# A sparse attention with a gated network behind it: the second chunk's exponentials stay in PSUM, four output buffers, and another order at two places

## The chip, the core and the metric

The kernel runs on one core of one Trainium2 chip. A core has five engines with a queue each: TensorE (PE, whose weight loads are listed as PEld), VectorE (DVE), ScalarE (ACT), GpSimd (POOL) and SyncE (SP). SP issues most of the DMA transfers, POOL some. The metric is the device time of one execution in microseconds (us), as a median over executions. PSUM is the memory that PE writes its results to, in banks of 128 partitions by 512 floats; SBUF is the large memory on the chip.

## The reference, cut to what matters

```python
# q, k, v: 8 batches x 8 heads x 576 positions x 64; 8 global positions
scores = scale * np.matmul(q, k.transpose(0, 1, 3, 2))
mask = np.abs(pos[:, None] - pos[None, :]) <= 32
mask = mask | is_global[:, None] | is_global[None, :]
scores = np.where(mask, scores, -1000000000.0)
attn = softmax(scores)
x = attn @ v                       # regrouped as 4608 tokens x 512
g = x @ w_gate                     # 512 -> 1536
ffn_out = gelu(g) * (x @ w_val) @ w_out
out = x + sigmoid(x @ w_res) * ffn_out
```

Each token attends to its neighbours within 32 positions and to 8 global positions; the global positions attend to all. The result goes through a gated network and is added back under a second gate.

## The kernel before

**Tiles and chunks.** The 4608 tokens are worked through in nine chunks (number c, 0 to 8) of 512, that is, eight windows of 64 query positions. A chunk has four token tiles (t, 0 to 3) of 128. For a chunk, the attention gives `xtok` (tokens by features), which is transposed into `xt` (`turn_x`, L591). The network is then computed from `xt`: for each of twelve blocks j of the hidden width, a gate product and a value product (`ffn_in`, L602; matmuls at L618), a Gelu on ACT (L624) and a product on DVE (L625) that gives `ht`. The output half (`ffn_out`, L629) has for each token tile a residual gate (L636, L639) and three thirds of the last product (L661). After the third one DVE forms `prb` (L665), POOL adds the tokens and gives `ob` (L667), and SP sends `ob` to the output (L669). The attention of chunk c + 1 is placed between the pieces of the output half of chunk c.

**What sets the order.** The order is written out by hand: instructions stand on each engine in the order in which the program names them, and every engine works its own list in order. Between engines there are waits: for an operand, or for a buffer that is still in use. Buffers of one tag take turns: `ob` and `prb` have two each, the PSUM tag "mm" four banks, the tag "sc" two banks, and the pair of banks "nd" exists once.

**The attention of a chunk.** `scores` (L533) computes for half of the windows (a "quad") four banks of scores, two from "sc" and two from "mm". `weigh` (L528) takes the exponential on ACT and writes it to `pt` in SBUF as bf16. `mask` (L543) multiplies `pt` by the window mask on DVE (L545). `local_values` (L551) multiplies `pt` with V into a value sum `nd`, `values` (L567) adds the part of the global positions (L575), which needs `vgs` from `global_rows` (L488, L503), and divides (L581 and L582 for tiles 0 and 2 of chunk 0, L587 and L588 else). In chunk 0 the mask is added by PE ahead of the exponential instead (`first_scores`, L508).

**The start (L732 to L773).** For chunk 0 the value sums of three tiles are begun ahead (`begun_v`), with a copy on ACT (L734) in between. Then values, transposes (`turn_x`) and the first two blocks of gate and value products take turns tile by tile; `begin(t)` is these products for tile t, 16 small matmuls that need the transposed tile t, which ACT copies out of PSUM (L599; DVE for tile 3).

**The end of chunk 0 (L853 to L894).** Here the attention of chunk 1 is placed between the output pieces of chunk 0 by hand. `third(t, n)` is one third of the output product of tile t. In the same place the K and Q of batch 2 are loaded (L199), cast (L205, K on ACT, Q on POOL) and transposed by DMA on SP (`turn_qk`, L461, five transfers for each of K and Q; `qt` and `kt` are their destinations).

**The next chunk.** At the beginning of chunk 1, SP transposes Q of batch 2, and POOL issues the loads of V (L99) and three indirect gathers of global rows of K, Q and V (`gather`, L326, issued at L328) into `kgf`, `qgf`, `vgf`. After block 9 the gathered K and Q are transposed on PE (`turn_globals`, L402, L407), after a cast on DVE (L397). After block 11, `global_scores` (L468) uses `qt` and `kt`. At block 8 POOL's loads of batch 3 into `q_st` and `k_st` are issued (`load_qk`, L87).

The last tile of all is finished by `ending` (L641) in three pieces of 256, 128 and 128 columns, each with its own `prb` (L650), `ob` (L653) and output transfer (L654).

Of the kernel before, what the change touches and what calls it, by code (L numbers as in the profile page):

```python
# [8 lines left out]
F32 = mybir.dt.float32  # L9
# [3 lines left out]
ACTF = mybir.ActivationFunctionType  # L13
ALU = mybir.AluOpType


def view(t, p0, pn, off, dims):

    step = t.ap[0][0]
    return bass.AP(tensor=t.tensor, offset=t.offset + p0 * step + off, ap=[[step, pn]] + dims)  # L20
# [3 lines left out]
def kernel(  # L24
# [12 lines left out]
    nc = tc.nc  # L37
# [4 lines left out]
    SCALE = 1.0 / float(D) ** 0.5  # L42
# [14 lines left out]
    work = ctx.enter_context(tc.tile_pool(name="work", bufs=2))  # L57
# [144 lines left out]
    def cast_second(what, r0, r1, copy):  # L202
        for r in range(r0, r1):
            n = min(128, S - 128 * r)
            copy({"q": q_st, "k": k_st}[what][0:n, r, :], place2[what][r][0:n, :])  # L205
# [255 lines left out]
    def turn_qk(b, parts="qk"):  # L461
        for what in parts:
            src, dst, c0 = (q_st, qt[b % 2], 0) if what == "q" else (k_st, kt[b % 2], 32)
            for r in range(NQT):
                n = min(128, S - 128 * r)
                nc.sync.dma_start(dst[:, :, c0 + 128 * r:c0 + 128 * r + n], src[0:n, r, :], transpose=True)
# [58 lines left out]
                                     qt[b % 2][64 * u:64 * u + 64, 2 * pp + m, 64 * i:64 * i + 64],  # L525
                                     start=first, stop=first or (m == 1 and n == 3))

    def weigh(quad, pp, u, sc):  # L528
        mine = view(pt, 0, 128, ((4 * pp + u) * CH + 4 * quad) * 128, [[2 * CH * 128, 2], [128, 4], [1, 64]])
        nc.scalar.activation(mine, sc, ACTF.Exp, bias=0.0, scale=SCALE)  # L530
        return mine

    def scores(c, quad):  # L533

        i0 = (CH * c + 4 * quad) % NW
        banks = []
        for pp, pool, tag in ((0, pss, "sc"), (1, psm, "mm")):
            sc = [pool.tile([128, 2, 4, 64], F32, name="sc", tag=tag) for _ in range(2)]
            heads(c, quad, pp, sc, True)
            banks += [(pp, u, sc[u]) for u in range(2)]  # L540
        mine = [weigh(quad, *which) for which in banks]

        def mask(n0, n1):  # L543
            for m in mine[n0:n1]:
                nc.vector.tensor_tensor(m, m, view(maskw, 0, 128, 64 * i0, [[0, 2], [64, 4], [1, 64]]), ALU.mult)  # L545
        return mask

    def split(c, t):
# [2 lines left out]
    def local_values(c, t):  # L551
        if split(c, t):
            nds = [psm.tile([128, 512], F32, name=f"nd{hf}", tag="mm") for hf in range(2)]
            nd = None
        else:
            nd = psn.tile([128, 2, 512], F32, name="nd", tag="nd")
            nds = [nd[:, 0, :], nd[:, 1, :]]
        wins = [divmod(CH * c + 2 * t + e, NW) for e in range(2)]
        for h in range(H):
            for e, (b, i) in enumerate(wins):  # L560
                vw = ve[b % 2][:, i // 2, h, :] if i % 2 == 0 else vo[b % 2][:, i // 2, h, :]
                c0 = (h * CH + 2 * t + e) * 128 - 64 * e
                nc.tensor.matmul(nds[h // 4][:, VG * (h % 4):VG * (h % 4) + VG],  # L563
                                 view(pt, 0, 128, c0, [[1, 128]]), vw, start=(h % 4 == 0 and e == 0), stop=False)
        return nd, nds, wins
# [25 lines left out]
    def turn_x(c, t):  # L591
        mine = xt[c % 2][:, :, 128 * t:128 * t + 128]
        if c > 1 and t < 3:
            nc.sync.dma_start(mine, xtok[c % 2][:, t, :], transpose=True)
            return
        tx = pss.tile([128, NKT, 128], BF16, name="tx", tag="sc")
        for kk in range(NKT):
            nc.tensor.transpose(tx[:, kk, :], xtok[c % 2][:, t, 128 * kk:128 * kk + 128], ident)
        (nc.vector.tensor_copy if c or t == 3 else nc.scalar.copy)(mine, tx)  # L599
# [29 lines left out]
    def ffn_out(c, t):  # L629

        held = {}

        def gate():
            r_ps = psm.tile([128, 512], F32, name="r_ps", tag="mm")
            for kk in range(NKT):
                nc.tensor.matmul(r_ps, xt[c % 2][:, kk, 128 * t:128 * t + 128], wr_t[:, kk, :],  # L636
                                 start=(kk == 0), stop=(kk == NKT - 1))
            held["r"] = work.tile([128, 512], BF16, name="rsb", tag="rsb", bufs=4)
            nc.scalar.activation(held["r"], r_ps, ACTF.Tanh, bias=0.0, scale=0.5)  # L639

        def ending():  # L641

            r0 = 512 * c + 128 * t
            for c0, c1 in ((0, 256), (256, 384), (384, 512)):
                f = psm.tile([128, 512], F32, name="f_ps", tag="mm")
                for j in range(NFF):
                    nc.tensor.matmul(f[:, 0:c1 - c0], ht[:, j, 128 * t:128 * t + 128], wo_t[:, j, c0:c1],
                                     start=(j == 0), stop=(j == NFF - 1))
                prb = work.tile([128, 512], F32, name="prb", tag="prb")
                nc.vector.scalar_tensor_tensor(prb[:, c0:c1], held["r"][:, c0:c1], 1.0, f[:, 0:c1 - c0],  # L650
                                               ALU.add, ALU.mult)
                ob = work.tile([128, 512], F32, name="ob", tag="ob")
                nc.vector.tensor_tensor(ob[:, c0:c1], prb[:, c0:c1], xtok[c % 2][:, t, c0:c1], ALU.add)  # L653
                nc.sync.dma_start(out[r0:r0 + 128, c0:c1], ob[:, c0:c1])  # L654

        def third(n):
            def emit():
                if n == 0:
                    held["f"] = psm.tile([128, 512], F32, name="f_ps", tag="mm")
                for j in range(4 * n, 4 * n + 4):  # L660
                    nc.tensor.matmul(held["f"], ht[:, j, 128 * t:128 * t + 128], wo_t[:, j, :],  # L661
                                     start=(j == 0), stop=(j == NFF - 1))
                if n == 2:
                    prb = work.tile([128, 512], F32, name="prb", tag="prb")
                    nc.vector.scalar_tensor_tensor(prb, held["r"], 1.0, held["f"], ALU.add, ALU.mult)  # L665
                    ob = work.tile([128, 512], F32, name="ob", tag="ob")
                    nc.gpsimd.tensor_tensor(ob, prb, xtok[c % 2][:, t, :], ALU.add)  # L667
                    r0 = 512 * c + 128 * t
                    nc.sync.dma_start(out[r0:r0 + 128, :], ob)  # L669
            return emit  # L670

        if c == NCH - 1 and t == 3:
            return [gate, ending, lambda: None, lambda: None]
        return [gate, third(0), third(1), third(2)]
# [57 lines left out]
    begun_v = [local_values(0, t) for t in range(2)]  # L732
    global_rows(0)
    ACT(vo[0][0:64, 2:4, :, :], ve[0][64:128, 2:4, :, :])  # L734
    begun_v.append(local_values(0, 2))

    nc.scalar.activation(none, none, ACTF.Gelu, bias=0.0, scale=1.0)
    for n in range(4):
# [18 lines left out]
    def begin(t):  # L757
        for steps in begun:
            for what in "gv":
                steps[what](128 * t, 128 * t + 128)  # L760

    values(0, 2, begun_v[2])
    turn_x(0, 0)
    values(0, 3)
    turn_x(0, 1)
    begin(0)
    turn_x(0, 2)
    begin(1)
    turn_x(0, 3)
    begin(2)  # L770
    begin(3)
# [8 lines left out]
    for c in range(NCH):  # L780
# [72 lines left out]
        if c == 0:  # L853
            def third(t, n):
                work_f[4 * t + 1 + n]()

            global_exp(1, *global_scores(1))
            work_f[0]()
            scores(1, 0)(0, 4)
            work_f[4]()  # L860
            work_f[8]()
            mask = scores(1, 1)
            work_f[12]()
            global_rows(1)
            for what in "kq":
                load_second(what)
            cast_second("k", 0, NQT, ACT)
            began = local_values(1, 0)
            third(0, 0)
            values(1, 0, began)  # L870
            mask(0, 2)
            third(1, 0)
            values(1, 1)
            mask(2, 4)
            third(2, 0)
            turn_x(1, 0)
            third(3, 0)
            values(1, 2)
            turn_x(1, 1)
            third(0, 1)  # L880
            cast_second("q", 0, 1, POOL)
            values(1, 3)
            third(1, 1)
            cast_second("q", 1, 3, POOL)
            turn_qk(2, "k")
            turn_x(1, 2)
            third(2, 1)
            third(3, 1)
            turn_x(1, 3)
            for t in range(4):  # L890
                third(t, 2)
                if t == 1:
                    cast_second("q", 3, NQT, POOL)
            continue  # L894
        jobs = {n: [] for n in range(16)}
        if c + 1 < NCH:
# [48 lines left out]
```

The softmax here doesn't subtract the row's maximum and nothing guards it: scores larger than these inputs give would overflow.

## Time and profile before

| | |
|---|---|
| median of eight executions | 402.37 us (400.34 to 403.74) |
| the profiled execution | 404.44 us |
| its span, first to last instruction | 402.7 us |
| mean granted clock of PE | 0.992 |
| HBM read and written | 39.19 MB, 9.44 MB |

A page of the profile describes one execution. It gives the busy time of each engine, the span in 40 slices, the chain of work that ended last (followed back from the last instruction to what released it), and the costliest groups of instructions by line. A row of a group has the line, the engine, the operation, its output and inputs, their shapes and how often it ran; behind the bar the busy time and the mean of one in ns, and the idle time of the engine just before it with what ended most of it. The chain's main lines are:

```profile
PE 72%; DMA 9%; POOL 6%; issue 5%; DVE 3%; ACT 3%; SPq 2%; POOLq 0%; DVEq 0%
```

A view in order of time has start, duration, engine, line, operation, operands and count; in brackets stands how long the engine was idle before and who ended that. The granted clock of PE is given as a share of full speed; at 0.50 every matmul takes about twice as long.

### The profile page before, as it was taken

The page shows a single profiled execution, that of the slowest core. Times are in us where ns is not written, and L with a number is a line of the kernel's source. Part 1 is how long each engine was busy: PE and PEld are TensorE (multiplying, and loading weights), DVE is VectorE, ACT ScalarE, POOL GpSimd, SP SyncE. Part 2 cuts the span into 40 slices and gives each one's busy share as a digit, 9 for nine tenths or more (in the row PEclk, how much of TensorE's full clock was granted, in tenths as well). Part 3 has the DMA queues.
Part 4 walks back from the last instruction along what each step waited for, and adds up shares of the span by engine and source line. Part 5 has one row for each costly group of instructions (what it writes and reads, how often), then busy time and mean ns, then how long its engine had stood idle before and what let it go on. Part 6 is the DMA issues. An engine that isn't in the chain of part 4 may idle for free.

```text
span 402.7 us, 8443 instructions
## 1 busy us (share of the span) xinstructions
PE 380.9 (95%) x3310; PEld 197.5 (49%) x3360; DVE 204.8 (51%) x445; ACT 168.3 (42%) x279; POOL 172.7 (43%) x207
## 2 busy tenths in 40 slices
PE   3989989997999999999999999999999999999995
PEld 2664545442554455445544554455445544554443
DVE  7758666533553455355545553565345634453422
ACT  6653574232623362337233633363336333633320
POOL 7877795497129712562286225722501110121011
PEclk9999999996999999999999999999999999999999
DMA  8999999599429992999399939993990310031002
GB/s 250 247 377 347 233 341 190 127 145 184 63 78 121 186 118 80 101 180 129 86 112 152 130 84 120 173 109 94 117 142 26 93 54 0 2 83 63 0 28 78
DMA packets 153003, 52.78 MB, mean 131 GB/s; under 512 B 136387, under 2 KB 143427, under 8 KB 152963
## 3 DMA queue, kind: packets, MB, share of 16 engines
q1 hardware_dynamic: 77024, 41.88, 44.9%
q0 software_dynamic: 75392, 9.84, 41.8%
q8 instruction: 26, 0.43, 0.5%
q10 hardware_dynamic: 546, 0.52, 0.4%
q14 instruction: 15, 0.11, 0.1%
HBM read 39.19 MB, written 9.44 MB: 121 GB/s over the span
## 4 chain that ended last, share of the span: by engine, by line
PE 72%; DMA 9%; POOL 6%; issue 5%; DVE 3%; ACT 3%; SPq 2%; POOLq 0%; DVEq 0%
PE v_ps L618 19%; PE g_ps L618 18%; PE f_ps L661 17%; PE r_ps L636 6%; PE nd L563 3%; DMA qgf<-in_q_dram,idx 3%; POOL ve L99 2%; PE sc L523 2%; DMA extra<-in_moe_w_out_dram 2%; POOL ob L667 2%; DMA kt<-k_st 2%; PE nd L575 2%; POOL wo_t L145 1%; DMA vraw<-in_q_dram 1%; SPq L199 1%
## 5 line engine op out<-in xcount | busy, mean ns | idle before, releaser
L625 DVE SCALAR_TENSOR_TENSOR ht<-gsb,v_ps 128x512 bf16<-128x512 bf16 x108 | 74.1, 687 | 99.5 <-PE v_ps L618 94.3
L624 ACT ACTIVATE gsb<-g_ps 128x512 bf16<-128x512 f32 x108 | 64.4, 597 | 130.5 <-PE g_ps L618 118.6
L667 POOL TENSOR_TENSOR ob<-prb,xtok 128x512 f32<-128x512 f32 x35 | 40.4, 1155 | 182.5 <-DVE prb L665 178.4
L618 PE MATMUL v_ps<-xt,wv_t 128*128 128x512 bf16 (+1 forms) x456 | 113.1, 371 | 0.6 <-issue 0.2
L618 PE MATMUL g_ps<-xt,wg_t 128*128 128x512 bf16 (+1 forms) x438 | 111.0, 371 | 0.8
L661 PE MATMUL f_ps<-wo_t,ht 128*128 128x512 bf16 x395 | 98.1, 379 | 1.8 <-issue 0.8
L618 PEld LDWEIGHTS <-wv_t 128*128 128x128 bf16 x456 | 43.8, 99 | 50.2 <-issue 2.1
L618 PEld LDWEIGHTS <-wg_t 128*128 128x128 bf16 x456 | 43.6, 99 | 50.4 <-issue 2.8
L661 PEld LDWEIGHTS <-ht 128*128 128x128 bf16 x420 | 38.8, 98 | 38.5
L639 ACT ACTIVATE rsb<-r_ps 128x512 bf16<-128x512 f32 x36 | 21.6, 606 | 71.1 <-PE r_ps L636 70.0
L530 ACT ACTIVATE pt<-sc 128x512 bf16<-128x512 f32 x72 | 37.5, 619 | 5.2 <-PE sc L523 5.2
L665 DVE SCALAR_TENSOR_TENSOR prb<-rsb,f_ps 128x512 f32<-128x512 bf16 x35 | 24.0, 685 | 28.3 <-PE f_ps L661 24.2
L636 PE MATMUL r_ps<-wr_t,xt 128*128 128x512 bf16 x137 | 36.2, 379 | 0.4
L545 DVE TENSOR_TENSOR pt<-pt,maskw 128x512 bf16<-128x512 bf16 x64 | 30.4, 488 | 8.3 <-ACT pt L530 6.3
L91 POOL DMA_DIRECT2D q_st<-in_q_dram x25 | 21.5, 868 | 15.8 <-DMA qt<-q_st 15.3
L563 PEld LDWEIGHTS <-pt 128*128 128x128 bf16 x576 | 21.9, 97 | 11.3 <-DVE xtok L588 2.4
L99 POOL DMA_DIRECT2D ve<-in_v_dram x30 | 25.5, 864 | 0.0
L588 DVE TENSOR_TENSOR xtok<-nd,rden 128x512 bf16<-128x512 f32 x34 | 23.5, 691 | 1.3
L563 PE MATMUL nd<-ve,pt 128*128 128x65 bf16 x320 | 23.1, 193 | 0.8 <-DVE xtok L588 0.6
L91 POOL DMA_DIRECT2D k_st<-in_k_dram x25 | 21.1, 856 | 5.7 <-DMA kt<-k_st 4.5
L563 PE MATMUL nd<-vo,pt 128*128 128x65 bf16 x256 | 20.2, 193 | 1.5 <-ACT vo L734 0.6
L587 DVE RECIPROCAL rden<-nd 128x8 f32<-128x8 f32 x34 | 7.0, 207 | 28.6 <-PE nd L575 28.5
(166 smaller groups left out, 294.2 us busy)
## 6 DMA issues: line engine op xcount, KB each, us to landing
out_dram<-ob SPq DMA_DIRECT2D x35, 256.0 KB, 2.1
vo<-ve SPq DMA_DIRECT2D x12, 260.0 KB, 5.2
q_st<-in_q_dram POOLq DMA_DIRECT2D x20, 128.0 KB, 5.3
k_st<-in_k_dram POOLq DMA_DIRECT2D x20, 128.0 KB, 6.3
ve<-in_v_dram POOLq DMA_DIRECT2D x18, 128.0 KB, 6.8
wo_t<-in_k_dram SPq DMA_DIRECT2D x8, 256.0 KB, 5.4
vraw<-in_q_dram SPq DMA_DIRECT2D x8, 256.0 KB, 6.8
extra<-in_moe_w_out_dram SPq DMA_DIRECT2D x4, 512.0 KB, 7.8
```

The lines of the kernel that those rows point to most:

```text
L91: nc.gpsimd.dma_start(dst[0:n, r, :].rearrange("p (h d) -> p h d", d=D), src[b].rearrange("h s d -> s h d")[128 * r:128 * r + n])
L99: nc.gpsimd.dma_start(t[p0:p1, c, :, 0:D], v[b].rearrange("h s d -> s h d")[s0 + p0:s0 + p1])
L530: nc.scalar.activation(mine, sc, ACTF.Exp, bias=0.0, scale=SCALE)
L545: nc.vector.tensor_tensor(m, m, view(maskw, 0, 128, 64 * i0, [[0, 2], [64, 4], [1, 64]]), ALU.mult)
L563: nc.tensor.matmul(nds[h // 4][:, VG * (h % 4):VG * (h % 4) + VG], view(pt, 0, 128, c0, [[1, 128]]), vw, start=(h % 4 == 0 and e == 0), st ...
L618: nc.tensor.matmul(held[what][:, c0:c1], w[:, kk, 128 * j:128 * j + 128], x[:, kk, c0:c1], start=(kk == 0), stop=(kk == NKT - 1))
L624: nc.scalar.activation(gsb, held["g"], ACTF.Gelu, bias=0.0, scale=1.0)
L625: nc.vector.scalar_tensor_tensor(ht[:, j, :], gsb, 0.5, held["v"], ALU.mult, ALU.mult)
L636: nc.tensor.matmul(r_ps, xt[c % 2][:, kk, 128 * t:128 * t + 128], wr_t[:, kk, :], start=(kk == 0), stop=(kk == NKT - 1))
L661: nc.tensor.matmul(held["f"], ht[:, j, 128 * t:128 * t + 128], wo_t[:, j, :], start=(j == 0), stop=(j == NFF - 1))
L665: nc.vector.scalar_tensor_tensor(prb, held["r"], 1.0, held["f"], ALU.add, ALU.mult)
L667: nc.gpsimd.tensor_tensor(ob, prb, xtok[c % 2][:, t, :], ALU.add)
```

## The change

Five edits, in two groups.

- For chunk 1 the exponential is written back into its PSUM bank as float, and the mask product reads it from there and writes `pt`. The masks of the second half are placed right behind its scores (two) and behind `global_rows` (two), instead of behind the values of tiles 0 and 1.
- `ob` has four buffers instead of two.
- The K transposes of batch 2 (`turn_qk(2, "k")`) are named after the outputs of tiles 0 and 1 of chunk 0, instead of ahead of all four.
- At the start, the value sum of tile 2 is not begun ahead any more; it is computed with its values, after those of tiles 0 and 1.
- `begin(0)` stands right after the transpose of tile 0, `begin(1)` right after that of tile 1, and `begin(2)` and `begin(3)` after those of tiles 2 and 3. Before, each of `begin(0)` and `begin(1)` had one more transpose ahead of it.

```diff
-    def weigh(quad, pp, u, sc):
+    def weigh(quad, pp, u, sc, stay=False):
         mine = view(pt, 0, 128, ((4 * pp + u) * CH + 4 * quad) * 128, [[2 * CH * 128, 2], [128, 4], [1, 64]])
-        nc.scalar.activation(mine, sc, ACTF.Exp, bias=0.0, scale=SCALE)
-        return mine
+        nc.scalar.activation(sc if stay else mine, sc, ACTF.Exp, bias=0.0, scale=SCALE)
+        return mine, sc if stay else mine
...
-        mine = [weigh(quad, *which) for which in banks]
+        mine = [weigh(quad, *which, stay=(c == 1)) for which in banks]
 
         def mask(n0, n1):
-            for m in mine[n0:n1]:
-                nc.vector.tensor_tensor(m, m, view(maskw, 0, 128, 64 * i0, [[0, 2], [64, 4], [1, 64]]), ALU.mult)
+            for m, x in mine[n0:n1]:
+                nc.vector.tensor_tensor(m, x, view(maskw, 0, 128, 64 * i0, [[0, 2], [64, 4], [1, 64]]), ALU.mult)
...
-                    ob = work.tile([128, 512], F32, name="ob", tag="ob")
+                    ob = work.tile([128, 512], F32, name="ob", tag="ob", bufs=4)
...
     ACT(vo[0][0:64, 2:4, :, :], ve[0][64:128, 2:4, :, :])
-    begun_v.append(local_values(0, 2))
...
-    values(0, 2, begun_v[2])
+    values(0, 2)
     turn_x(0, 0)
+    begin(0)
     values(0, 3)
     turn_x(0, 1)
-    begin(0)
+    begin(1)
     turn_x(0, 2)
-    begin(1)
     turn_x(0, 3)
     begin(2)
     begin(3)
...
             mask = scores(1, 1)
+            mask(0, 2)
             work_f[12]()
             global_rows(1)
+            mask(2, 4)
...
             values(1, 0, began)
-            mask(0, 2)
             third(1, 0)
             values(1, 1)
-            mask(2, 4)
             third(2, 0)
...
             cast_second("q", 1, 3, POOL)
-            turn_qk(2, "k")
             turn_x(1, 2)
...
                 third(t, 2)
                 if t == 1:
                     cast_second("q", 3, NQT, POOL)
+                    turn_qk(2, "k")
```

## The prediction, made before the changed kernel had run

> **What bounds the kernel now.** I read the busy shares first, then the stretches with the granted clock, then the chain of waits around the stretch that stands out, then each engine in order of time.
>
> ```profile
> PE 380.9 (95%) x3310; PEld 197.5 (49%) x3360; DVE 204.8 (51%) x445; ACT 168.3 (42%) x279; POOL 172.7 (43%) x207
> ```
>
> TensorE is the bound. Other engines matter only where they make PE wait, or make it run slowly. By stretch (start and end, length, busy time of PE, PEld, DVE, ACT, POOL, granted clock, DMA share, GB/s):
>
> ```profile
> 72.60:90.00 17.40, 17.35 (x82) 7.84 (x80) 7.48 (x11) 5.90 (x10) 12.43 (x15) 1.00 1.00 135
> 90.00:93.50 3.50, 0.59 (x3) 0.10 (x1) 0.32 (x2) 0.07 (x1) 2.70 (x3) 0.89 1.92 168
> 93.50:99.50 6.00, 5.59 (x14) 2.20 (x16) 2.49 (x10) 0.97 (x2) 5.79 (x8) 0.50 1.99 196
> ```
>
> At 90 us, in chunk 1, PE stands for 3 us, and then works for 6 us at half clock. The row of granted clocks shows no other such place. The chain of waits says who did it (start, length, what):
>
> ```profile
> 77.12 2.23 DMA out_dram<-ob
> ...
> 79.48 0.58 POOL ob L667
> ...
> 80.59 1.16 POOL ob L667
> 81.75 4.25 POOL ve L99 x5
> ...
> 86.31 1.07 POOL kgf L328
> ...
> 87.68 5.70 DMA qgf<-in_q_dram,idx
> ...
> 93.69 0.29 PE tg L407
> 93.97 1.71 PE g_ps L618 x4
> ```
>
> POOL's third output sum of chunk 0 needs one of two output buffers. It is free only when an output has landed (79.35). The loads of V and the gathers queue behind it on POOL, and PE's transposes of the gathered rows (L407) end the chain. That output was late because of SP's queue:
>
> ```profile
> 70.08 6.94 SPq L466 DMA_TRANSPOSE kt<-k_st  x5
> 77.12 4.99 SPq L669 DMA_DIRECT2D out_dram<-ob  x4
> 82.16 6.61 SPq L466 DMA_TRANSPOSE qt<-q_st  x5
> ```
>
> The first sum was ready at 73.2, but its output stood behind five K transposes until 77.1. POOL waited 4.05 us for it.
>
> What it costs: PE's last matmul before the hole ends its issue at 90.14 (89.28 plus four at 0.216). Two transposes (0.11), two pairs of gate and value products (4 x 0.864 = 3.46) and the usual 0.1 before the global scores would bring those to 93.81. They start at 100.18. So 6.37 us are lost: 3.5 of standing, 2.85 of half clock (four products in 6.3 instead of 3.46).
>
> **The change, part by part.**
>
> *Four buffers, and two outputs ahead of the K transposes.* The third sum no longer waits for an output. POOL's order is unchanged: two sums, two casts of Q (end 75.4), two sums. The sums follow PE, which will be 1.25 us later here (below), so they run at 72.45 to 74.75, the casts to 75.95, the other sums to 78.25; with V loads (4.3 us), the K gather is issued at 82.85 instead of 86.31. Its landing took 6.4, the Q gather's 5.7: both have landed by 89.9, their casts (0.23) are done by 90.2, and PE asks at 91.4. The wait goes with 1.2 to spare.
> On SP, outputs 0 and 1 leave at 73.7 and 74.8, the K transposes run 75.2 to 82.1 (before: from 70.1), outputs 2 and 3 (0.35 each) follow, and the Q transposes start at 82.9 instead of 82.16, the last one at 88.2. Their landings took 5.7 to 6.9, so the last is there at 93.9 to 95.1. **That is what is late next**: the global scores read them, and PE, without its hole, arrives at 90.14 + 1.25 + 3.67 = 95.05. I count 0.2 of waiting. K's are 5 us later, and at 6.4 each still landed by 88. Behind the Q transposes stand POOL's reloads of the Q staging: 5 Q and 5 K loads, 8.6 us of issue with the last Q landing at 95, done near 100; POOL's next sum comes at about 101.5.
>
> *The tail.* The last token tile writes three outputs through the same buffers:
>
> ```profile
> 399.14 0.29 DVE L653 TENSOR_TENSOR ob<-prb,xtok 128x128 f32<-128x128 f32 x1 [0.86 <-DMA out_dram<-ob]
> 399.35 0.28 DVE L650 SCALAR_TENSOR_TENSOR prb<-rsb,f_ps 128x128 f32<-128x128 bf16 x1
> 399.91 0.29 DVE L653 TENSOR_TENSOR ob<-prb,xtok 128x128 f32<-128x128 f32 x1 [0.28 <-DMA out_dram<-ob]
> ```
>
> Both waits vanish with four buffers. PE's last matmul is issued by 398.4, so the last sum starts at 398.93 instead of 399.91: **-0.97**, all on the path.
>
> *The start of the first products (17 to 30 us).* Two edits. The values of tile 2 leave the place where they covered a wait for a copy; that wait (0.63) becomes one for DVE's row of value sums (ready 21.36), and the vector work of tile 0 starts 0.42 earlier. But each group of first products now follows directly on its own transpose, without another group between them. The copy in between is
>
> ```profile
> 23.72 0.59 ACT L599 COPY xt<-tx 128x512 bf16<-128x512 bf16 x1 [0.88 <-PE tx L598]
> ```
>
> about 0.84 from PE's last transpose to PE's next matmul. Step by step: transpose 0 ends 23.09, products 0 start 23.93; their last PSUM bank is freed by the division of tile 2 at 24.85, so they end 25.13 (0.3 lost); tile 3's values and transpose 1 end 26.07; products 1 run 26.9 to 27.8; transposes 2 and 3 end 28.24; products 2 and 3 run 28.85 to 30.6. Before, they ended at 29.17: **+1.4**. PE is gapless from 30 to 48 (19.80 busy of 20), so nothing absorbs it. No new gap is over 0.84 (an estimate from these rows); gaps of up to 0.63 left the clock at 1.00 in this stretch, longer ones it doesn't show, so a tripped clock is priced in a rival.
>
> *Exponentials that stay in PSUM, masks moved ahead.* Eight exponentials write to PSUM; no row has that, so ACT's cost is bounded by -0.1 and +0.1 each around 0.52 (four in 2.09); I take 0. Masks:
>
> ```profile
> 53.25 4.08 DVE L545 TENSOR_TENSOR pt<-pt,maskw 128x512 bf16<-128x512 bf16 x4 [0.52 <-ACT pt L530]
> 57.26 0.69 DVE L503 TENSOR_TENSOR vgs<-sn,head 128x520 bf16<-128x520 f32 x1
> 59.09 0.21 DVE L587 RECIPROCAL rden<-nd 128x8 f32<-128x8 f32 x1 [1.15 <-PE nd L575]
> 59.39 0.69 DVE L588 TENSOR_TENSOR xtok<-nd,rden 128x512 bf16<-128x512 f32 x1
> ```
>
> The Trainium skill (VectorE: DVE Perf Modes, the perf-mode tier table) speaks against this edit: a tensor_tensor on two bf16 operands in SBUF runs twice as fast as one with a PSUM operand. By that, from the 0.47 of a mask in chunk 1 (1.90 for four) to 0.69: 8 x 0.22 = +1.8 us of DVE. But in this stretch the eight masks take 4.08 + 2.02 + 1.17 = 7.27, or 0.91 each, while POOL is busy; a product with one PSUM input takes 0.69 in the same stretch. Eight at 0.69 are 5.5: **-1.75 of DVE**. I take the row.
>
> What PE gets of it: the banks are now held until the mask. Masks 0 to 3 end at 53.94, 54.64, 55.3, 56.0; the second half's score matmuls, before at 54.13 and 54.74, start at 54.7 and at 55.4 to 56.1; the global rows wait for mask 4 (57.05, before 56.21); tile 1's values wait for the division of tile 0 behind all masks: 60.8 instead of 60.14. From there PE has no mask in the way: the waits of 0.52 and 0.2 and late reciprocals go, and the second transposes come at about 64.4 as before, tile 3's values at 65.5 instead of 65.67. **-0.15** in sum, between -0.8 (all four mask and division waits go) and +1.1 (the bank wait stays).
>
> Sum at the global scores: -6.37 + 1.4 - 0.15 + 0.2 = -4.9; tail -0.97; **-5.9**. Later chunks move as a whole.
>
> **From the sum to the time.** The profiled execution took 404.44; so 398.5 by its own. It lies above all eight runs shown (400.34 to 403.74, median 402.37). The half clock may be the reason. The skill (TensorE: Matmul & The Clock Gate, "What's actually happening") has the clock halved after an idle window of about 3.4 us that runs freely. By that rule a gap of 2.7 need not trip it; here the row shows that it did, with 6 us at 0.50. If the phase decides, the other runs lose 0 to 2.85 where this one lost all. Taking away 5.9 from the median gives 396.5, taking away only the 3.05 that doesn't depend on the clock gives 399.3. I take **398.0**.
>
> **Rivals.**
> - *Q lands late* (0.20). K and Q transposes, V loads and gathers now share some 15 us of DMA, whose share was already 1.00 to 1.99. A landing 2 us later makes PE wait 2: 400. For it: kt landed in 2.5 alone, qt in 6.4 among loads. Against: issue, at 1.33 each, doesn't depend on it.
> - *Banks held longer, gaps at the start dearer* (0.13): +1.1 at the masks instead of -0.15, the gaps 1 more: 398.0 + 2.3 = 400.3; up to 402.5 if one of them trips the clock.
> - *The gathers don't come earlier* (0.05): then the hole stays, -0.97 + 1.25: 402.6.
> - *Slower* (0.07): the wait for Q at the global scores becomes a hole of its own. From 2.7 us on it halves the clock as the old hole did (+2.85), and then the result is 398.0 + 2.7 + 2.85 = 403.6, slower than before; at 4 us it is 404.9. That needs a Q landing of 9.6 us and more; none of the five took over 6.9.
> - *As forecast* (0.55): 396.3 to 399.7.
>
> A measurement here tells about 0.5% (2 us) from no change. The forecast is faster; the first rival about half so, the second too; the third is no change. That gives 0.67, 0.24, 0.09. Range: from 395.8 (the full half clock in every run, masks at -0.8) to 401.4, into the first two rivals.
>
> **What would show it.** PE's wait on the cast of the gathered keys (2.7) gone and the clock 1.00 near 90 us; POOL's 4.1 wait on the output gone; no wait in the tail's sums; PE gaps of about 0.8 before products 0, 1 and 2, and the first full product about 1.4 later; L545 near 0.69. Wrong, if the global scores wait over 1 us for Q, or a stretch at half clock appears elsewhere.

## The result, and the profile after

| | before | after |
|---|---|---|
| median | 402.07 us | 397.34 us (twelve executions, 396.21 to 400.51) |
| profiled execution | 404.44 us | 400.19 us |
| its span | 402.7 us | 398.5 us |
| its mean granted clock | 0.992 | 0.996 |

The medians lie 4.7 us or 1.2% apart. The ratio on record, which isn't formed from the two medians, is 0.9901 (95%: 0.9878 to 0.9925), so the changed kernel is faster by about 1%. The before column's median comes from 33 executions on the same chip as those of after, so it differs a little from the 402.37 above; one of them, at 659.44 us, is far outside the rest and is left out of the ratio. Of the twelve, ten lie between 396.21 and 398.93, with a clock of 0.999 or 1.00; two, with 0.996, lie at 400.15 and 400.51. Of two further ones, the profiled execution is like these two, and the other took 397.38. The trace of the profiled execution therefore shows something that most executions don't have, and a second trace of the same program is used beside it below (r1_again).

The page of after, its busy shares and then the shares of the chain of waits by engine:

```profile
PE 378.9 (95%) x3310; PEld 197.5 (50%) x3360; DVE 204.1 (51%) x445; ACT 168.4 (42%) x279; POOL 170.7 (43%) x207
...
PE 84%; DVE 5%; DMA 4%; issue 3%; ACT 2%; POOL 2%; DVEq 0%; SPq 0%; POOLq 0%
```

PE has risen from 72% of the chain to 84%, and DMA has fallen from 9% to 4%. The same three stretches of chunk 1 as before (columns as there):

```profile
72.60:90.00 17.40, 17.30 (x83) 8.03 (x84) 7.99 (x12) 4.53 (x8) 12.90 (x14) 1.00 0.93 131
90.00:93.50 3.50, 3.50 (x18) 1.57 (x16) 1.70 (x4) 1.24 (x3) 1.23 (x2) 1.00 0.83 179
93.50:99.50 6.00, 5.95 (x68) 2.86 (x68) 3.36 (x10) 3.60 (x7) 6.00 (x8) 1.00 1.47 165
```

In the second stretch PE is busy 3.50 of 3.50 us where it was busy 0.59, and in the third the clock is 1.00 where it was 0.50. The hole is gone. SP's queue and POOL's in order of time show how:

```profile
76.07 1.47 SPq L669 DMA_DIRECT2D out_dram<-ob  x2
78.14 6.57 SPq L466 DMA_TRANSPOSE kt<-k_st  x5
84.80 1.01 SPq L669 DMA_DIRECT2D out_dram<-ob  x2
85.87 7.34 SPq L466 DMA_TRANSPOSE qt<-q_st  x5
```

```profile
74.89 2.27 POOL L667 TENSOR_TENSOR ob<-prb,xtok 128x512 f32<-128x512 f32 x2 [4.25 <-DVE prb L665]
77.10 1.16 POOL L205 CAST q_st<-vraw 128x512 bf16<-128x512 f32 x2
78.23 2.26 POOL L667 TENSOR_TENSOR ob<-prb,xtok 128x512 f32<-128x512 f32 x2
80.44 4.31 POOL L99 DMA_DIRECT2D ve<-in_v_dram  x5
85.06 1.07 POOL L328 DMA_INDIRECT kgf<-in_k_dram,idx  x1 [0.30 <-issue]
```

The first two outputs leave ahead of the K transposes. The third and fourth sums follow the casts with no wait at all; before, the third waited 4.05 us for an output. The K gather takes 5.8 us to land and the Q gather, issued at 86.44, 4.9, so both are there by 91.4. PE's own list:

```profile
93.77 0.22 PE L407 MATMUL tg<-ident,kgd 128*128 128x128 bf16 x1
...
97.42 0.43 PE L472 MATMUL sg<-qt,kgz 128*32 128x288 bf16 x8
```

No bracket stands behind either row: PE waits neither for the gathered rows nor, at the global scores, for Q. These scores start at 97.42 instead of 100.18.

### The profile page after: what moved, and what is told of

Read it like the earlier page. It is cut to its first block, busy times and chain, and to the rows that moved or that the text cites. A ratio compares the mean times of both kernels' runs of the same rounds, so it can differ in the third digit from the quotient of the medians.

```text
span 398.5 us, 8434 instructions
## 1 busy us (share of the span) xinstructions
PE 378.9 (95%) x3310; PEld 197.5 (50%) x3360; DVE 204.1 (51%) x445; ACT 168.4 (42%) x279; POOL 170.7 (43%) x207
## 4 chain that ended last, share of the span: by engine, by line
PE 84%; DVE 5%; DMA 4%; issue 3%; ACT 2%; POOL 2%; DVEq 0%; SPq 0%; POOLq 0%
PE v_ps L618 21%; PE f_ps L661 20%; PE g_ps L618 20%; PE r_ps L636 7%; PE nd L563 4%; PE sc L523 3%; PE nd L575 2%; DMA kt<-k_st 2%; DMA vgf<-in_v_dram,idx 2%; PE ss L477 1%; POOL ve L99 1%; DVE gt L486 1%; PE sg L472 1%; PE tx L598 1%; PE sc L512 1%
## 5 line engine op out<-in xcount | busy, mean ns | idle before, releaser
L618 PE MATMUL v_ps<-xt,wv_t 128*128 128x512 bf16 (+1 forms) x456 | 111.9, 368 | 0.6
L618 PE MATMUL g_ps<-xt,wg_t 128*128 128x512 bf16 (+1 forms) x438 | 109.5, 367 | 2.6 <-ACT xt L599 1.8
L636 PE MATMUL r_ps<-wr_t,xt 128*128 128x512 bf16 x137 | 37.1, 386 | 0.3
L530 ACT ACTIVATE pt<-sc 128x512 bf16<-128x512 f32 x64 | 33.3, 614 | 5.2 <-PE sc L523 5.2
L545 DVE TENSOR_TENSOR pt<-pt,maskw 128x512 bf16<-128x512 bf16 x56 | 23.2, 424 | 7.8 <-ACT pt L530 5.8
L636 PEld LDWEIGHTS <-xt 128*128 128x128 bf16 x144 | 13.5, 98 | 15.3 <-issue 0.5
```

The source lines that it names most:

```text
L530: nc.scalar.activation(sc if stay else mine, sc, ACTF.Exp, bias=0.0, scale=SCALE)
L618: nc.tensor.matmul(held[what][:, c0:c1], w[:, kk, 128 * j:128 * j + 128], x[:, kk, c0:c1], start=(kk == 0), stop=(kk == NKT - 1))
```

## The experiments

Each ratio is to the kernel before on the same chip, with its 95% interval. The medians come from several chips, on which the kernel before had medians from 401.52 to 402.53, so differences below 1 us between two runs are also read from their traces below. In the texts that were written ahead of a run, "the look" is its profiled execution. The first four experiments ask what took the hole away, the next two what the start costs, then four what the masks do.

| label | median us (range) | ratio (95%) |
|---|---|---|
| q1_bufs | 397.02 (395.94 to 397.14) | 0.9849 (0.9813 to 0.9886) |
| q2_order | 397.86 (397.67 to 398.42) | 0.9876 (0.9840 to 0.9913) |
| q3_both | 397.68 (396.52 to 400.04) | 0.9879 (0.9838 to 0.9920) |
| p1_k_first | 397.40 (396.22 to 398.18) | 0.9882 (0.9842 to 0.9922) |
| s1_old_start | 396.26 (395.12 to 396.64) | 0.9826 (0.9788 to 0.9863) |
| s2_late_tile2 | 395.68 (395.48 to 398.00) | 0.9836 (0.9803 to 0.9870) |
| m1_masks_sbuf | 400.44 (399.14 to 402.55) | 0.9971 (0.9952 to 0.9990) |
| m2_masks_as_before | 397.95 (397.15 to 398.43) | 0.9892 (0.9858 to 0.9926) |
| r1_again (after itself) | 397.55 (397.10 to 400.21) | 0.9904 (0.9867 to 0.9940) |
| g1_rows_psum | 397.56 (397.20 to 398.50) | 0.9886 (0.9851 to 0.9920) |
| b1_sum | 396.54 (395.43 to 397.10) | 0.9862 (0.9823 to 0.9901) |
| b2_sum_k_first | 396.63 (396.24 to 398.50) | 0.9878 (0.9838 to 0.9919) |

### Buffers or order: q1, q2, q3, p1

q1_bufs is the kernel before with four output buffers and nothing else (the line stands twice; the one in `ending` is shown):

```diff
-                ob = work.tile([128, 512], F32, name="ob", tag="ob")
+                ob = work.tile([128, 512], F32, name="ob", tag="ob", bufs=4)
```

> Four output buffers alone, in the kernel before. Theory (the gain is the hole at 90 us, which POOL's third sum causes by waiting for an output buffer): the third sum starts at about 75.4 instead of 79.5, the gathers land before PE asks, the hole and its half clock go (3.5 to 6.4 us), and the tail loses 1 us: 396, between 394.7 and 397.6. Rival (the gain comes from the masks of chunk 1): only the tail changes, 401.

The SP and the POOL queue of q1_bufs, in order of time:

```profile
69.82 6.94 SPq L466 DMA_TRANSPOSE kt<-k_st  x5
76.86 1.99 SPq L669 DMA_DIRECT2D out_dram<-ob  x4
```

```profile
75.33 2.26 POOL L667 TENSOR_TENSOR ob<-prb,xtok 128x512 f32<-128x512 f32 x2
...
82.16 1.07 POOL L328 DMA_INDIRECT kgf<-in_k_dram,idx  x1 [0.30 <-issue]
```

The outputs stand behind the K transposes as before (76.86), and yet the third sum runs at 75.33, ahead of any output, and the gather is issued at 82.16 instead of 86.31. PE meets its transposes of the gathered rows at 89.83 without a wait. So the late output did harm only through the buffer that it held. The buffers alone bring the whole kernel from 402.53 (the median before in this comparison) to 397.02, at least as much as the entire change does.

q2_order is the kernel before with the K transposes moved and two buffers:

```diff
             cast_second("q", 1, 3, POOL)
-            turn_qk(2, "k")
             turn_x(1, 2)
...
                     cast_second("q", 3, NQT, POOL)
+                    turn_qk(2, "k")
```

> Only the two outputs moved ahead of the K transposes, two output buffers, in the kernel before. Theory: the first output lands at about 75.8, so that the third sum waits 0.3 us instead of 4.05, and the hole goes too, the tail stays as it was: 397, between 395.7 and 398.6. Rival (only buffers help, since SP is no faster): 402. If both this and the buffers alone remove the hole, either of them would have been enough.

The order alone removes the hole too: the third sum runs at 75.16, the gather is issued at 82.02. What it leaves is the tail. DVE's last sums in q2_order:

```profile
392.51 0.29 DVE L653 TENSOR_TENSOR ob<-prb,xtok 128x128 f32<-128x128 f32 x1 [0.87 <-DMA out_dram<-ob]
...
393.28 0.29 DVE L653 TENSOR_TENSOR ob<-prb,xtok 128x128 f32<-128x128 f32 x1 [0.27 <-DMA out_dram<-ob]
```

These are the two waits of before (0.86, 0.28) again. The 0.84 us between the medians of q1 and q2 agrees with them in size, though the intervals overlap.

q3_both has both edits; p1_k_first is the changed kernel with the K transposes back ahead of the outputs, that is, the diff of q2_order undone, with its four buffers kept.

> Buffers and order together in the kernel before, without the edits of the start and of the masks. Theory: 396, no better than the buffers alone, and about 1.4 below the changed kernel (397.3) if the masks give nothing. Rival (the masks give a part): 397 or more.

> The changed kernel with the K transposes ahead of all outputs, as before; four buffers stay. Theory: with four buffers POOL waits for no output, so the order on SP is worth nothing: 397.0 to 397.6, as in the changed kernel, the gathers' issue unchanged. Rival (the order is what brings the gathers forward): the hole is back, 400 or more.

q3_both is no faster than q1_bufs (397.68 and 397.02), as expected, but the 396 was missed: it lies where its rival had it, level with the changed kernel. p1_k_first is no slower than the changed kernel (397.40 and 397.34 to 397.55). In p1_k_first the third and fourth sums run at 75.45 and the gather is issued at 82.28; the hole doesn't come back (PE waits 0.28 for the gathered Q). With four buffers the place of the K transposes is worth nothing that the medians show.

### The start: s1, s2

s1_old_start is the changed kernel with the old start; s2_late_tile2 keeps the late values of tile 2, and puts only the products back to their old places. The diff of s1, against after (s2 has the same without its two lines on `begun_v`):

```diff
+    begun_v.append(local_values(0, 2))
...
-    values(0, 2)
+    values(0, 2, begun_v[2])
     turn_x(0, 0)
-    begin(0)
     values(0, 3)
     turn_x(0, 1)
-    begin(1)
+    begin(0)
     turn_x(0, 2)
+    begin(1)
     turn_x(0, 3)
```

> The changed kernel with the start of before (tile 2's values begun ahead, first products one transpose behind). Theory: the edit of the start costs 1.4 us, so 395.9, and the first product of full width is issued 1.46 us earlier than in the changed kernel. Rival (the later stages absorb it): 397.3.

> The changed kernel with the first products one transpose behind, as before, but tile 2's values late, as in the change. Theory: the cost of 1.46 is that of the copy from PSUM between a transpose and its products, and the late tile 2 in itself gains about 0.4: first full product at about 28.8, 395.5. Rival (the late tile 2 costs, through the banks that the first products wait for): 396.3 or more, no better than the start of before.

PE's rows of the first products, in after:

```profile
23.95 0.38 PE L618 MATMUL g_ps<-xt,wg_t 128*128 128x128 bf16 x4 [0.67 <-ACT xt L599]
...
26.92 0.38 PE L618 MATMUL g_ps<-xt,wg_t 128*128 128x128 bf16 x4 [0.67 <-ACT xt L599]
...
28.87 0.38 PE L618 MATMUL g_ps<-xt,wg_t 128*128 128x128 bf16 x4 [0.45 <-ACT xt L599]
```

and in s2_late_tile2, the transpose of tile 1 with the products of tile 0 right behind it, which need an earlier transpose:

```profile
24.39 0.38 PE L598 MATMUL tx<-ident,xtok 128*128 128x128 bf16 x4
24.61 0.39 PE L618 MATMUL g_ps<-xt,wg_t 128*128 128x128 bf16 x4
```

The three waits for the copy (0.67, 0.67, 0.45) are in the first and not in the second. What they cost is read best from a point ahead of both edits, the last products of the global rows (L501), to the first full product (of 512 columns). In before, after and s2_late_tile2, in this order:

```profile
20.16 0.46 PE L501 MATMUL sn<-ve,ptg 128*16 128x130 bf16 x20
29.38 1.02 PE L618 MATMUL g_ps<-xt,wg_t 128*128 128x512 bf16 x3
```

```profile
20.18 0.46 PE L501 MATMUL sn<-ve,ptg 128*16 128x130 bf16 x20
30.84 1.02 PE L618 MATMUL g_ps<-xt,wg_t 128*128 128x512 bf16 x3
```

```profile
20.01 0.46 PE L501 MATMUL sn<-ve,ptg 128*16 128x130 bf16 x20
28.81 1.02 PE L618 MATMUL g_ps<-xt,wg_t 128*128 128x512 bf16 x4
```

That is 9.22, 10.66 and 8.80 us. The traces of all fourteen kernels fall into these three groups, to 0.01: 9.22 to 9.23 with the old start (before, q1, q2, q3, s1), 10.66 to 10.67 with the new one (after, r1, p1, m1, m2, g1), 8.79 to 8.80 with the products at their old places and tile 2 late (s2, b1, b2). So the new places of the products cost 1.86 us, and the late values of tile 2 gain 0.42, as s2's expectation had it; the edit of the start loses the difference, 1.44. The medians of s1 and s2 both lie over 1 us below after's, but don't tell the two apart (396.26 and 395.68).

### The masks: m1, m2, r1, g1

m1_masks_sbuf is the changed kernel with the masks in their new places, but with the exponentials written to SBUF again:

```diff
-        mine = [weigh(quad, *which, stay=(c == 1)) for which in banks]
+        mine = [weigh(quad, *which, stay=False) for which in banks]
```

> The changed kernel, but the exponentials of chunk 1 go to SBUF as before; the masks keep their new places. Theory (a product with a PSUM operand is not held up by POOL, one with two SBUF operands is): L545 takes about 0.9 in chunk 1 instead of 0.64, the global rows' product and tile 0's division come later, 398.3 and more spread. Rival (what PSUM costs is the banks, held until the mask): faster than the changed kernel, 396.8.

The loss came, and it was larger than expected: 400.44, 3.1 above the changed kernel. DVE in m1_masks_sbuf:

```profile
53.58 1.67 DVE L486 TENSOR_TENSOR gt<-gt,maskr 128x576 bf16<-128x576 bf16 x1 [1.60 <-ACT gt L485]
55.17 6.29 DVE L545 TENSOR_TENSOR pt<-pt,maskw 128x512 bf16<-128x512 bf16 x6
61.38 0.68 DVE L503 TENSOR_TENSOR vgs<-sn,head 128x520 bf16<-128x520 f32 x1
```

Six masks take 1.05 us each, and the row of value sums (L503) stands behind all six. It comes 2.2 us later than in an ordinary execution of the changed kernel (59.22 in r1_again, below); 0.9 of that is L486, which takes 1.67 here and 0.78 there. PE's value matmuls wait for it, and from 62 to 65 us the clock is 0.50:

```profile
62.12 0.81 PE L575 MATMUL nd<-vgs,gt 128*128 128x260 bf16 x3 [1.62 <-DVE vgs L503]
```

With both operands in SBUF, the masks in their new places cost 2.5 us against the old places (397.95 in m2_masks_as_before, same chip); moved there, they have to read PSUM.

m2_masks_as_before undoes the mask edits altogether: that line, and the two `mask` calls back behind `values(1, 0)` and `values(1, 1)`.

```diff
-            mask(0, 2)
             work_f[12]()
             global_rows(1)
-            mask(2, 4)
...
             values(1, 0, began)
+            mask(0, 2)
             third(1, 0)
             values(1, 1)
+            mask(2, 4)
```

> The changed kernel with the masks entirely as before (SBUF, old places). Theory: the mask edits together are worth about 0.6 us when POOL doesn't hold up another product, so 397.9. Rival (masks give nothing, or cost through the product that POOL held up for 2.8 us): 397.3 or less, and no execution at 400.

397.95 is 0.4 to 0.6 above the two medians of the changed kernel, with overlapping intervals. The traces don't make it clearer. From the first full product of chunk 0 to the second transpose of chunk 1's tokens it is 34.51 us in m2, and 34.45 in r1_again; but with the same old masks it is 35.04 in before and in q1. PE's waits for masks differ between these (in before and q1 one of 0.52 that m2 lacks). So the mask edits gain between 0.06 and 0.6, according to the execution that they are compared with (more against q3, with 35.91, where PE also waits 0.55 for POOL's casts).

r1_again is the changed kernel once more (an empty line moves its line numbers by one), for a second trace and more executions.

> The changed kernel once more, word for word but for an empty line. What is open is how often an execution falls to 400. Theory (POOL's casts hold up the product L486 in some executions, 3 of 12 so far): median 397.3, some at 400; where the look shows the product short, the stretch from the global scores of batch 1 to the second transpose lasts about 14.6 us instead of 17.25.

One of its eight executions took 400.21, with a clock of 0.996; the others 397.10 to 398.20, at 0.999 or more. The trace is of an ordinary one; from the global scores to the second transpose it takes 14.49 us, where 14.6 was expected, against 17.25 in after's profiled execution. Here are DVE and POOL in the attention of chunk 1, first of after's profiled execution, then of r1_again:

```profile
53.73 2.80 DVE L486 TENSOR_TENSOR gt<-gt,maskr 128x576 bf16<-128x576 bf16 x1 [1.60 <-ACT gt L485]
56.45 3.67 DVE L545 TENSOR_TENSOR pt<-sc,maskw 128x512 bf16<-128x512 f32 x6
```

```profile
53.63 0.61 POOL L190 CAST ve<-wo_t 96x512 bf16<-96x512 f32 x1
54.19 2.02 POOL L145 CAST wo_t<-extra 128x1024 bf16<-128x1024 f32 x2
```

```profile
53.97 0.78 DVE L487 TENSOR_TENSOR gt<-gt,maskr 128x576 bf16<-128x576 bf16 x1 [1.60 <-ACT gt L486]
54.95 2.48 DVE L546 TENSOR_TENSOR pt<-sc,maskw 128x512 bf16<-128x512 f32 x4 [0.20 <-ACT sc L531]
```

```profile
53.83 0.61 POOL L191 CAST ve<-xtok 128x512 bf16<-128x512 f32 x1
54.39 0.84 POOL L191 CAST ve<-wo_t 96x512 bf16<-96x512 f32 x1
```

The mask product of the global rows (L486, L487 in r1_again; both inputs in SBUF as bf16) starts in both traces inside a cast on POOL. In r1_again it ends 0.31 after that cast (54.44), and the next cast takes 0.84 instead of some 0.6. In after it ends 0.32 after the third cast in a row (56.21). In m1_masks_sbuf it ends 0.32 after the second (55.25 and 54.93). In q1, q2, q3, s2 and m2 it also starts inside an instruction of POOL, and ends 0.30 to 0.32 after that one. In before it starts at 52.27 as a copy of POOL ends (52.28): it takes 0.46, and the next copy 0.90 instead of 0.62. So it is a wait until POOL is through, and in after two casts that began later went ahead of it. The Trainium skill says as much (SBUF — State Buffer, "Who interferes with whom" and the notes on the two sides ahead of it): VectorE and GpSimd share a pair of ports, an instruction with two SBUF inputs on the one side excludes a GpSimd instruction that reads SBUF for its whole length, and the loser waits. The ends agree with that. The page also gives the ports to whichever starts first; the two casts that went ahead in after don't agree with it. What decides who goes first is not shown.

The six masks behind it, with one input in PSUM, took 0.61 each beside POOL's casts in after, and 0.62 in r1_again. They don't wait for POOL. But in after they begin 1.5 us later than in r1_again, and PE's score matmuls need the banks that they free:

```profile
57.18 0.19 PE L523 MATMUL sc<-qt,kt 64*128 64x64 bf16 x1 [1.52 <-DVE pt L545]
57.77 0.41 PE L523 MATMUL sc<-qt,kt 64*128 64x64 bf16 x16 [0.41 <-DVE pt L545]
```

By stretch, in after:

```profile
53.00:58.00 5.00, 2.81 (x55) 1.61 (x56) 4.27 (x4) 4.14 (x9) 4.76 (x8) 1.00 1.05 391
58.00:59.00 1.00, 0.81 (x29) 0.47 (x22) 1.00 (x3) 0.81 (x2) 1.00 (x2) 0.81 1.15 318
59.00:60.00 1.00, 1.00 (x4) 0.30 (x2) 1.00 (x2) 1.00 (x3) 1.00 (x2) 0.50 1.31 239
```

PE is busy 2.81 of 5 us (3.98 in r1_again), and then runs at half clock for some 3.4 us, up to 62. In r1_again the clock is 1.00 throughout. From the first full product of chunk 0 to the second transpose of chunk 1's tokens it is 35.04 us in before (29.38 to 64.42), 34.45 in r1_again and 37.21 in after's profiled execution: 2.8 us between two executions of one program. The executions with a clock of 0.996 lie about as far above the others.

g1_rows_psum keeps the exponentials of the global rows of chunk 1 in PSUM as well, so that L486's product has only one input in SBUF:

```diff
+        if b == 1:
+            nc.scalar.activation(sg[:, :, 0:288], sg[:, :, 0:288], ACTF.Exp, bias=0.0, scale=SCALE)
+            nc.vector.tensor_tensor(g.rearrange("p (a c) -> p a c", a=2), sg[:, :, 0:288],
+                                    maskr.rearrange("p (a c) -> p a c", a=2), ALU.mult)
+            return
```

> The changed kernel, and for batch 1 also the exponentials of the global rows stay in PSUM until their mask product (L486). In the profile after, this product with two SBUF operands took 2.8 us beside POOL's casts, with a hole in PE and half clock behind it. Theory: with a PSUM operand it takes about 0.75 in every execution, the executions at 400 vanish, median 397.0, none above 398.5. Rival (the executions at 400 have another cause, such as the phase of the clock): some of them stay at 400.

The product takes 0.76 in its trace, as expected; the median, 397.56, is that of the changed kernel and not 397.0. No execution of this edit was at 400: none of 17 with the two runs below. Without it, four of 22 of the changed kernel were (fourteen of after, eight of r1_again): the profiled one, the two of the twelve, and one of r1_again. But s1, s2 and p1 have the old product and had none in 18 either, and q3_both, which has the old masks, had one at 400.04 with a clock of 0.991. So that this product causes all of the long executions is argued from one trace; the runs do not settle it.

### The sum: b1, b2

b1_sum joins the start of s2_late_tile2 and the edit of g1_rows_psum; b2_sum_k_first adds the order of p1_k_first.

> The changed kernel with the first products one transpose behind, tile 2's values late, and the global rows' exponentials in PSUM. Theory: as s2_late_tile2 (395.7), and without executions held up at L486: 395.5, none above 397. Rival (the two don't add up): 396 or more.

> As b1_sum, with the K transposes ahead of all outputs. Theory: the order on SP is worth nothing either way, 395.5 within 0.4 of b1_sum. Rival (K transposes sooner are of use to the global scores): below b1_sum by more than 0.5.

The 395.5 expected of both was missed, and the rival named for b1 (the two don't add up) came; b2 lies as close to b1 as expected. Neither is below s2_late_tile2 (396.54 and 396.63 against 395.68), and all three intervals overlap. The traces show why an earlier start isn't worth its full size. POOL must cast the Q of batch 2 ahead of the first output sum, and its loads don't land earlier for an earlier start; `prb` has only two buffers, and DVE's third `prb` waits for that sum. In s2's profiled execution, the slowest of its six (398.00):

```profile
71.09 0.61 POOL L205 CAST q_st<-vraw 128x512 bf16<-128x512 f32 x1 [5.66 <-DMA vraw<-in_q_dram]
...
75.78 1.02 PE L618 MATMUL g_ps<-xt,wg_t 128*128 128x512 bf16 x4 [1.82 <-DVE prb L665]
```

From the second transpose to the global scores it is 29.38 us in g1, m1, m2, q1, q2, q3 and r1 (29.37 in after), but 30.15 in s1, 30.16 in b1, 30.05 in b2 and 31.66 in s2 (29.83 in p1, with its wait for the gathered Q). The best versions found are the changed kernel with the old places of the products, s2_late_tile2 (0.9836) and s1_old_start (0.9826); what is added in b1 and b2 is not told apart from nothing.

## Why the prediction was right, step by step

The forecast was 398.0 us, and the median is 397.34. The case named as likeliest came, by the mechanism given for it. How near the number came is partly luck: 398.0 was picked between the 396.5 and 399.3 that the two readings of the clock gave. And one term of the sum was wrong by more than its bounds in some executions.

**The hole: right, but only half of its stated cause was needed.** The 2.7 of waiting for the gathered keys, the half clock behind it and POOL's 4.05 are all gone, as said. In r1_again POOL's sums start at 72.37 and the K gather is issued at 82.54, where 72.45 and 82.85 were forecast; in after's profiled execution both are over 2 us later, because PE is. The prediction told the buffers and the order as one step; q1 and q2 show that each is enough, and q3 and p1 that the second adds nothing.

**How much of it depends on the clock: rightly left open.** The prediction left open whether all executions of before lose the 2.85 us of half clock. Of 51 executions of before in the three comparisons, 36 had a clock of 0.996 or less (one at 0.997 is counted with the others) with a median of 402.7 us, and 15 had more with 400.2. q1 and q2, which lack the hole, have 0.998 or more in all twelve. So some seven in ten executions of before had half clock there. But most had less of it than the profiled one: that one has 0.992 with 6.8 us at half clock, after's profiled one has 0.996 with 3.4; of the 36, 31 are at 0.995 or 0.996 and five lower. By these two traces, an estimate, most lost about half of the 2.85. The medians differ by 2.5, so something else differs too. Taken from the median of before, the hole was thus worth less than the 6.37 of the profiled execution, which was among the longest. q2_order, which takes it away and leaves the tail, gains 4.7 over the median before of its comparison (402.53).

**Q at the global scores: no wait, where 0.2 was counted.** PE arrives without one. The first rival (0.20) did not come. For the gathered rows the prediction had 1.2 to spare. The Q gather landed in 4.9 instead of 5.7, at 91.34, 2.4 ahead of PE's transposes (93.77). But it left out DVE's own list, where the casts stand behind the product of the block:

```profile
92.31 0.69 DVE L625 SCALAR_TENSOR_TENSOR ht<-gsb,v_ps 128x512 bf16<-128x512 bf16 x1 [1.04 <-PE v_ps L618]
92.91 0.33 DVE L397 CAST kgd<-kgf 128x128 bf16<-128x128 f32 x1
93.05 0.27 DVE L397 CAST qgd<-qgf 128x128 bf16<-128x128 f32 x1
```

They end at 93.24 and 93.32, so 0.45 was left.

**The tail: right.** The last two sums in after:

```profile
395.13 0.29 DVE L653 TENSOR_TENSOR ob<-prb,xtok 128x128 f32<-128x128 f32 x1
...
395.66 0.29 DVE L653 TENSOR_TENSOR ob<-prb,xtok 128x128 f32<-128x128 f32 x1
```

No wait is left. From the first matmul of the last token tile's last product to the end of the span it is 6.09 us (7.11 before): -1.02, predicted -0.97.

**The start: right, in both of its parts.** The first full product comes 1.44 later, against +1.4: 1.86 for the new places less 0.42 for the late tile 2, the 0.42 by which the prediction had DVE's work start earlier. The three gaps are there (0.67, 0.67 and 0.45, where about 0.8 each was named), and the lost 0.3 for a PSUM bank too. The 19.80 busy of 20 us belong to the stretch from 30 to 50, not to 48. s1 gives 1.1 in medians.

**The masks: the row was the right one to take; the term held in ordinary executions, and failed in the profiled one.** Eight masks took 4.95 us of DVE in after (3.67 and 1.28) and 5.05 in r1_again, against a predicted 5.5; by the tier table they should have become dearer. The exponentials that write PSUM cost what those that write SBUF did, four of them in ACT's list of after:

```profile
54.06 2.08 ACT L530 ACTIVATE sc<-sc 128x512 f32<-128x512 f32 x4
```

For PE, the sum had -0.15, between -0.8 and +1.1. In r1_again the stretch from the first full product to the second transpose is 0.59 shorter than in before, but only 0.06 shorter than in m2, which has the old masks; both are within the bounds, and the runs don't fix the size. In after's profiled execution it is 2.17 longer than in before, outside them. The step that failed there is "**-0.15** in sum, between -0.8 (all four mask and division waits go) and +1.1 (the bank wait stays)". It priced the masks and said nothing of the product ahead of them, L486, which took 0.46 in the trace of before because it started between two of POOL's copies. Now the PSUM banks are held until the masks behind it are done, so what holds it up reaches PE through them. The second rival had 400.3 with a range up to 402.5 for banks held longer and a tripped clock; four of 22 executions lie there, at 400.15 to 400.51, and in the one of them that was traced the delay begins at L486. The sign that the prediction had named for being wrong, a stretch at half clock elsewhere, is there in that trace.

The profiled execution adds up so: the hole -6.37, the start +1.46 (0.02 of it from ahead of the edits), the attention of chunk 1 +2.17, the tail -1.02, in sum -3.8; measured is -4.2 of span. The other 0.4 lies between the global scores and the last tile's last product (295.41 us in before, 294.99 in after); over all fourteen traces that stretch varies from 294.65 to 295.61, and it was not traced further.

## What to carry to other kernels

Where an engine waits for a buffer that a transfer has yet to free, look at what stands ahead of that transfer in its queue, and try more buffers first: they cure the wait wherever it occurs, here at the tail too, while a new order cures one place. A step that is moved closer to what it depends on shows the whole time of the copy between; keep one independent group of matmuls between a transpose and its use. When results stay in PSUM until a vector product has read them, every instruction ahead of that product on its engine becomes part of how long the banks are held; price it with what it can be made to wait for, not with its usual row.

## What the runs showed of the hardware that was not expected

- One product of 0.46 us took 2.80 us by standing behind three casts of POOL in a row. All eight of this product in after, as duration in ns (least, median, most) with first and last start:

```profile
L486 DVE TENSOR_TENSOR gt<-gt,maskr x8: 457/459/2797, 18.7 to 303.2; 128x576 bf16<-128x576 bf16 x8
```

- The clock was halved behind a PE gap of 1.52 us with two of 0.41 and 0.19 close behind it (2.81 us busy of 5). The prediction had weighed the Trainium skill's idle window of about 3.4 us (TensorE: Matmul & The Clock Gate, "What's actually happening"); neither this gap nor the 2.7 us of before is as long, and both were followed by half clock. The gaps of 0.45 to 0.67 at the start left the clock at 1.00, and so did the one of 1.82 in s2_late_tile2 (2.09 us busy of 4, from 73 to 77): the longest gap doesn't decide by itself. What does was not measured.
- An exponential of 128x512 from PSUM back to PSUM as float cost 0.52, the same as to SBUF as bf16.
